# The first batch of a fused attention and expert kernel: which keys come as f32, who issues the hop, and in what order the tensor engine works

## The chip, the cores and the metric

The kernel runs on one core of a Trainium2 chip. Its time is the device time of one launch in microseconds (us). Three runs of the kernel before gave 668.44, 668.48 and 668.60 us; the median, 668.48 us, is the time before.

Five engines have instruction queues of their own: PE (TensorE, matrix multiplies; weight loads beside them), DVE (VectorE), ACT (ScalarE), POOL (GpSimd) and SP (SyncE, which only issues transfers here). POOL issues transfers too. An engine works through its queue in order; an instruction that waits for a semaphore holds everything behind it on that engine.

## The reference, cut to what matters

Two parts in a row. The first is a block-sorted attention for 4 batches of 8 heads with 768 tokens of 64 numbers each: five Sinkhorn rounds turn an 8x8 matrix per head into mixing weights `P`, these mix the 8 blocks (96 tokens each) of keys and values, and every block of queries attends to the mixed block at its own place. The second part is a mixture of 8 experts whose routing weights come from eight Sinkhorn rounds over all 3072 tokens.

```python
for _ in range(5):                       # P = sort_net, (B, H, 8, 8)
    P = exp(P - max(P)); P /= sum(P, -1); P /= sum(P, -2)
k_sorted = einsum('bhij,bhjcd->bhicd', P, k_blocks)   # the same for v
attn = softmax(q_b @ k_sorted_b.T / 8)   # block by block, 96 x 96
x = (attn @ v_sorted_b) as (3072, 512)   # tokens x (heads * 64)
P = routing(x @ w_gate)                  # 8 Sinkhorn rounds over (3072, 8)
out = sum over e of P[:, e] * (relu(x @ w1[e]) @ w2[e])
```

## The kernel before, in words

The batches of the attention are worked one after the other, and the hidden layer and output of expert 0 fill PE beside them (to about 107 us). The experts 1 to 7 follow in one long stage. The order of PE's work is written out by hand: `pin` keeps an instruction in program order on its engine, and strings of short step names are the plan. What is not pinned is placed by the scheduler of the framework.

Batch 0 (to about 36 us) has its own functions, which work on pairs of heads `hp` (0 to 3) and on halves `b` of the eight blocks (blocks 0 to 3 and 4 to 7):

- **Loads.** POOL issues the casting loads (f32 in memory, bf16 on the chip), `load_batch` and `load_w1` (L70 to L102), in the order queries, values, keys of heads 0 to 3, gate weights, first part of `w1`. The keys of heads 4 to 7 are loaded by SP as f32 into a corner of a later buffer (`rawk`, L68) and cast by ACT between the Sinkhorn rounds (L442).
- **Sinkhorn, L437 to L457**: DVE and ACT in turn. `Prep` (L460) copies the result 16 times side by side, split over DVE (4 rows of blocks), ACT (2) and POOL (2); `spread` sends it through PE to 128 partitions; `build_r` (L134) multiplies it with a mask on DVE, four pieces of two heads, giving the weights `Rt`.
- **Values.** `sort_pair` (L272) mixes the values of two heads on PE; DVE or ACT copies them to `vs`. The **hop** (L151) moves `vs` to `vsbt`, so that the 96 tokens of a block stand on 96 partitions: one transfer ("piece") per block, for all 8 heads or for 4. SP issues four pieces (block 0 in two halves, blocks 4 and 5), POOL eight (blocks 1 to 3 in two halves, blocks 6 and 7).
- **A gate.** Behind its last piece POOL copies two numbers out of the arrived pieces of blocks 0 and 1 (L482), and only then issues the next loads: two parts of `w1`, the values of batch 1, and, after the weights of batch 1, its keys and queries, `w2` and the loads of batch 2.
- **Keys, scores, mixes, turns.** `wide_keys` (k) mixes keys, copied by ACT for pairs 0 and 1 and by DVE for pairs 2 and 3; `half_scores` (s) makes scores, ACT takes the exponentials; `half_mix` (m) multiplies with the hopped values, DVE divides (a reciprocal of the sums, then a product into `og`); `half_turn` (t) transposes two pairs; `half_hidden` (h, g) are the two halves of expert 0's hidden layer on these tokens; `v0` to `v3` are `sort_pair` for batch 1, and `l` the routing logits. In the plan at L492 the two digits behind s and m are the half and the pair; behind t, h and g the half and a group. `m10` is thus the first mix that reads blocks 4 to 7, and it reads all four of them.
- **Blank matmuls.** `warm` (L325) multiplies a block of zeros to keep PE busy; the table `unread` says before which steps one stands.
- **PSUM.** All these steps share four buffers (`pair`); a step waits until the copy that reads its buffer's last content is done.

The later batches use `attention` (L364) with a plan of steps q, k, s, m, t, l: `usual` (L577) for batches 2 and 3, woven with expert 0. In batch 2 a step `x0`, a subtraction on DVE for later, stands behind each of q2, q3 and t0.

Of the kernel before, what the change touches and what calls it, by code (L numbers as in the profile page):

```python
# [20 lines left out]
def mkap(t, dims, off=0):  # L21
    return bass.AP(tensor=t.tensor, offset=t.offset + off, ap=dims)
# [3 lines left out]
def kernel(  # L26
# [11 lines left out]
    nc = tc.nc  # L38
    B, H, S, D = 4, 8, 768, 64
    NB, BL = 8, 96  # L40
    N, Dm, E, F = 3072, 512, 8, 1024
# [22 lines left out]
    pin = tc.keep_in_program_order  # L64
    kt, vt, qt = {}, {}, {}
    osbl = {0: xtp.tile([128, 18, Dm], F32, name="osbl0")}
    rawk = osbl[0].rearrange("p t d -> p (t d)")[:, 0:1536].rearrange("p (h x) -> p h x", h=4)
    nc.sync.dma_start(out=rawk, in_=k[0, 4:8].rearrange("h (p kk) d -> p h (kk d)", kk=6))  # L68

    def load_batch(bb, parts):  # L70
        for x, l0, n in parts:
# [24 lines left out]
    load_batch(0, [("q", l0, 4) for l0 in (0, 4)])  # L96
    Ibig = ones.tile([128, 128], BF16)
    make_identity(nc, Ibig)
    load_batch(0, [("v", 0, 4), ("v", 4, 4), ("k", 0, 4)])
    wg = ones.tile([128, 4, E], BF16)  # L100
    pin(nc.gpsimd.dma_start(out=wg, in_=moe_w_gate.rearrange("(kk k) e -> k kk e", k=128)))
    load_w1(0, 0, 384)  # L102
# [6 lines left out]
    VW = NB * 520  # L109
    vsbt = [perp.tile([128, VW], BF16, name=f"vsb{n}") for n in range(2)]  # L110
# [23 lines left out]
    def build_r(bb, eng, n, pbps=None):  # L134

        Rt[bb] = perp.tile([128, 8, 8, 16], BF16, name=f"R{bb % 2}")
        for h in range(0, 8, n):
            ins = eng.tensor_tensor(
                out=mkap(Rt[bb], [Rt[bb].ap[0], [16, 8 * n], [1, 16]] if pbps is None else
                         [Rt[bb].ap[0], [128, n], [16, 8], [1, 16]], off=h * 128),  # L140
                in0=(mkap(Pb, [Pb.ap[0], [1, 8 * n], [0, 16]], off=(bb * 8 + h) * 8)
                     if pbps is None else
                     mkap(pbps, [pbps.ap[0], [1, n], [32, 8], [0, 16]], off=h)),
                in1=mkap(mask16, [mask16.ap[0], [0, 8 * n], [1, 16]] if pbps is None else
                         [mask16.ap[0], [0, n], [0, 8], [1, 16]]),
                op=ALU.mult)
            if eng is nc.gpsimd:
                pin(ins)


    def hop(bb, pieces=None):  # L151
        for eng, i, h0, n in pieces or [(nc.gpsimd if i % 2 and bb > 1 else nc.sync, i, 0, 8)
# [116 lines left out]
        if 3 in ks:  # L269
            nc.vector.tensor_copy(glog[:, bb * TB:(bb + 1) * TB, :], gp[bb])  # L270

    def sort_pair(bb, hp, pair):  # L272
        t = pair()
        warm(t, bb == 0 and hp == 0)
        for h in range(2):
            pin(nc.tensor.matmul(t[:, h, 0:384], Rt[bb][:, 2 * hp + h].rearrange("p i c -> p (i c)"),
                                 vt[bb][:, 2 * hp + h, :], start=True, stop=True))
        (nc.vector.tensor_copy if (hp % 2 == 0 if bb else hp % 2) else nc.scalar.copy)(
            vs[:, :, 2 * hp:2 * hp + 2, 0:64],
            t[:, :, 0:384].rearrange("p h (kk d) -> p kk h d", d=64))  # L280

    def wide_queries(hp, pair):
        qT[0, hp] = sp.tile([128, 128, 6], BF16, name="qTs", bufs=4)
# [144 lines left out]
    with tc.tile_pool(name="ps0", bufs=4, space=bass.MemoryType.PSUM,  # L428
                      reuse_waits="tile") as ps0:
        pair = lambda: ps0.tile([128, 2, 512], F32, name="pair")  # L430
        warm(pair(), 11)
        rs = pp.tile([32, 8], F32)
        cs = pp.tile([32, 8], F32)
        Pt = P.rearrange("p i j -> p j i")
        nc.vector.reduce_max(out=rs, in_=P, axis=AX.X)
        nc.vector.tensor_sub(P, P, mkap(rs, [rs.ap[0], rs.ap[1], [0, 8]]))
        for it in range(5):  # L437


            pin(nc.scalar.activation(out=P, in_=P, func=AF.Exp))  # L440
            if it in (1, 2):
                pin(nc.scalar.copy(kt[0][:, 2 * it + 2:2 * it + 4], rawk[:, 2 * it - 2:2 * it]))  # L442
            if it == 3:
                warm(pair(), 3)
            for hp in {3: (0, 1), 4: (2, 3)}.get(it, ()):
                wide_queries(hp, pair)
            if it == 1:
                pin(nc.vector.reduce_sum(out=mask16, in_=Ibig.rearrange("p (j c) -> p c j", c=16),
                                         axis=AX.X))
            pin(nc.vector.reduce_sum(out=rs, in_=P, axis=AX.X))  # L450
            nc.vector.reciprocal(out=rs, in_=rs)
            nc.vector.tensor_mul(P, P, mkap(rs, [rs.ap[0], rs.ap[1], [0, 8]]))
            nc.vector.reduce_sum(out=cs, in_=Pt, axis=AX.X)
            if it == 0:
                nc.vector.tensor_scalar_add(cs, cs, 1e-9)
            nc.vector.reciprocal(out=cs, in_=cs)
            nc.vector.tensor_mul(Pt, Pt, mkap(cs, [cs.ap[0], cs.ap[1], [0, 8]]))  # L457

        Prep = perp.tile([32, 8, 8, 16], BF16, name="R1")
        for eng, i0, n in ((nc.vector.tensor_copy, 0, 4), (nc.scalar.copy, 4, 2),  # L460
                           (nc.gpsimd.tensor_copy, 6, 2)):
            pin(eng(Prep[:, i0:i0 + n], mkap(P, [P.ap[0], [8, n], [1, 8], [0, 16]], off=i0 * 8)))

        def spread(n):
            t = pair()
            warm(t, n)
            pbps = t[:, 0, 0:256].rearrange("p (i g) -> p i g", i=8)
            for i in range(8):
                pin(nc.tensor.matmul(pbps[:, i, :], Prep[:, i].rearrange("p j c -> p (j c)"),
                                     Ibig[0:32, 0:32], start=True, stop=True))  # L470
            return pbps

        build_r(0, nc.vector, 2, spread(9))
        S_, G_ = nc.sync, nc.gpsimd
        for hp in range(4):
            sort_pair(0, hp, pair)
            if hp == 1:
                hop(0, [(S_, 0, 0, 4), (G_, 1, 0, 4), (G_, 2, 0, 4), (G_, 3, 0, 4)])
        wide_keys(0, pair)
        hop(0, [(S_, 0, 4, 4), (G_, 1, 4, 4), (G_, 2, 4, 4), (G_, 3, 4, 4),  # L480
                (S_, 4, 0, 8), (S_, 5, 0, 8), (G_, 6, 0, 8), (G_, 7, 0, 8)])
        gate = nc.gpsimd.tensor_copy(  # L482
            held, mkap(vsbt[0], [[VW, 96], [520, 2]], off=259))
        with tc.issue_after(gate.ins):
            load_w1(0, 384, 640)
            load_w1(0, 640, F)
            load_batch(1, [("v", 0, 8)])
        wide_keys(1, pair)
        halves = [mps.tile([128, 8, 384], BF16, name="hTs") for _ in range(2)]
        unread = {"s03": 1, "m01": 1, "m02": 1, "m03": 1}  # L490
        part = {}
        for x in ("s00 k2 s01 k3 p s02 s03 m00 s10 m01 s11 m02 t00 m03 s12 m10 t01 s13 h00 m11 "  # L492
                  "g00 m12 h01 g01 m13 t10 h02 g02 t11 h03 g03 v0 v1 v2 v3 h10 g10 l").split():
            n = [int(c) for c in x[1:]]
            if x[0] == "s":
                half_scores(*n, pair, unread.get(x, 0))
            elif x[0] == "m":
                half_mix(*n, pair, unread.get(x, 0))
            elif x[0] == "t":
                half_turn(*n, lambda: ps0.tile([128, 2048], BF16, name="pair"),  # L500
                          nc.vector.tensor_copy if x == "t11" else nc.scalar.copy)
            elif x[0] == "h":
                part[x[1:]] = t = pair()
                half_hidden(*n, (0, 1), t)
            elif x[0] == "g":
                b, g, t = *n, part[x[1:]]
                half_hidden(b, g, (2, 3), t)
                nc.scalar.activation(out=halves[b][:, 2 * g:2 * g + 2, 0:384],
                                     in_=t[:, :, 0:384], func=AF.Relu)
            elif x[0] == "v":  # L510
                sort_pair(1, *n, pair)
            elif x[0] == "k":
                wide_keys(*n, pair)
            elif x[0] == "l":
                logits(0, lambda shape, dt: pair()[:, 0, 0:TB * E].rearrange(
                    "p (t e) -> p t e", e=E), range(4))
            else:
                nc.vector.tensor_copy(Pb, spread(0).rearrange("p i g -> p g i"))
                build_r(1, nc.gpsimd, 4)
                load_batch(1, [("k", 0, 8), ("q", 0, 4), ("q", 4, 4)])  # L520
                load_w2(0)
        hop(1)
# [10 lines left out]
    with ExitStack() as c2:  # L533
# [36 lines left out]
                                  "m0 m1,t0 m2,t1 m3,t2 t3,l0 l3")  # L570
        run_both(at1, (1, 1, 1, 0, 1, 0, 0, 1, 0, 1, 0, 2))
        load_batch(2, [(x, 0, 8) for x in "vkq"])
        build_r(2, nc.gpsimd, 4)
        run_both(at1, (2, 1, 1, 1))
        run_both(sort_values(2, bank1), (1, 0, 1, 0, 1))
        run_both(at1, (1, 1))
        usual = "q0,q1,k0 k1,q2,s0 k2,q3,s1 m0 k3,s2 m1,t0 s3 m2,t1 m3 t2 t3,l0 l3"  # L577
        for bb, ns in ((2, (5, 3, 2, 4)), (3, (5, 4, 0, 5))):
            at1 = attention(bb, bank1, usual if bb == 3 else usual.replace(
                "q2", "q2,x0").replace("q3", "q3,x0").replace("t0", "t0,x0"))  # L580
            weave(at1, ex, 5, ns[0])
            if bb + 1 < B:
                load_batch(bb + 1, [(x, 0, 8) for x in "vkq"])
                build_r(bb + 1, nc.gpsimd, 4)
            else:
                load_w1(1)
                sums = sum_w(1)
# [338 lines left out]
```

## Time and profile before

The profiled execution took 668.62 us, 0.14 us over the median; its span from the first to the last instruction is 666.9 us.

| what | value |
|---|---|
| PE busy | 654.7 us, 98% of the span |
| DVE, ACT, POOL busy | 535.6, 300.3, 472.6 us |
| PE's granted clock | full in every slice |
| PE busy from 12 to 25 us | 11.47 of 13.00 us |
| PE busy from 25 to 36 us | 10.95 of 11.00 us |
| PE busy from 36 to 107 us | 70.29 of 71.00 us |
| PE busy from 107 us on | 552.60 of 559.90 us |
| hop pieces of batch 0, issue to landing | 2.4 to 3.9 us, median 3.2 |
| hop pieces of batch 1, issue to landing | 5.6 to 7.6 us, median 6.4 |

A line of the timeline reads: start, length, engine, line of the source, operation, what it writes and reads, shapes, number of instructions, and in brackets how long the engine was idle before and what ended that. The chain of waits is followed back from the last instruction; a stretch on it is on the path that sets the end. DMA queue q0 holds what POOL issues, q1 what SP issues.

### The profile page before, as it was taken

The page shows a single profiled execution, that of the slowest core. Times are in us where ns is not written, and L with a number is a line of the kernel's source. Part 1 is how long each engine was busy: PE and PEld are TensorE (multiplying, and loading weights), DVE is VectorE, ACT ScalarE, POOL GpSimd, SP SyncE. Part 2 cuts the span into 40 slices and gives each one's busy share as a digit, 9 for nine tenths or more (in the row PEclk, how much of TensorE's full clock was granted, in tenths as well). Part 3 has the DMA queues.
Part 4 walks back from the last instruction along what each step waited for, and adds up shares of the span by engine and source line. Part 5 has one row for each costly group of instructions (what it writes and reads, how often), then busy time and mean ns, then how long its engine had stood idle before and what let it go on. Part 6 is the DMA issues. An engine that isn't in the chain of part 4 may idle for free.

```text
span 666.9 us, 13213 instructions
## 1 busy us (share of the span) xinstructions
PE 654.7 (98%) x5063; PEld 434.4 (65%) x5140; DVE 535.6 (80%) x1128; ACT 300.3 (45%) x535; POOL 472.6 (71%) x501
## 2 busy tenths in 40 slices
PE   7999999999999999999999999999999999999997
PEld 3766675554666666666666666666666666666666
DVE  6656876874888888888888888888888888888886
ACT  5775773476455433343333333333433343434330
POOL 4814343037897898898897999689886999646653
PEclk9999999999999999999999999999999999999999
DMA  9998964003042140033003040024003120001124
GB/s 187 175 220 143 149 109 64 1 0 64 1 64 42 24 64 0 1 64 48 17 1 64 2 64 1 11 53 64 1 1 65 20 45 1 1 0 61 68 95 159
DMA packets 33311, 36.96 MB, mean 55 GB/s; under 512 B 2112, under 2 KB 26304, under 8 KB 33248
## 3 DMA queue, kind: packets, MB, share of 16 engines
q0 software_dynamic: 26832, 27.13, 26.0%
q1 hardware_dynamic: 6416, 8.99, 4.3%
q8 instruction: 40, 0.66, 0.4%
q14 instruction: 23, 0.19, 0.1%
HBM read 52.45 MB, written 6.29 MB: 88 GB/s over the span
## 4 chain that ended last, share of the span: by engine, by line
PE 92%; DVE 2%; DMA 2%; ACT 2%; issue 1%; POOL 0%; ACTq 0%; DVEq 0%; POOLq 0%
PE oacc L766 37%; PE bk L678 36%; PE bk L392 3%; PE oacc L401 3%; PE bank L401 3%; PE bank L392 2%; PE bank L240 1%; DMA kvq<-in_q_dram 1%; DVE osbl L731 1%; PE pair L360 1%; DVE h L725 1%; PE bank L200 1%; PE bk L766 1%; ACT hT L721 1%; PE bank L251 1%
## 5 line engine op out<-in xcount | busy, mean ns | idle before, releaser
L731 DVE SCALAR_TENSOR_TENSOR osbl<-oacc,glog,osbl 128x256 f32<-128x256 f32 (+1 forms) x490 | 248.5, 521 | 61.9 <-PE oacc L766 61.9
L678 PE MATMUL bk<-xtT,w1e 128*128 128x512 bf16 x475 | 154.8, 379 | 0.9
L749 POOL TENSOR_TENSOR hs<-hT 128x512 bf16<-128x512 bf16 (+2 forms) x105 | 99.4, 956 | 63.0 <-DVE hT L718 62.9
L766 PEld LDWEIGHTS <-hT 128*128 128x128 bf16 x996 | 97.4, 98 | 62.8 <-issue 0.6
L766 PEld LDWEIGHTS <-hs 128*128 128x128 bf16 x996 | 96.9, 97 | 55.5 <-issue 0.2
L721 ACT ACTIVATE hT<-bk 128x512 bf16<-128x512 f32 x84 | 50.2, 598 | 159.3 <-PE bk L678 141.5
L766 PE MATMUL oacc<-w2e,hT 128*128 128x256 bf16 x796 | 119.6, 273 | 0.5
L749 POOL TENSOR_TENSOR hs<-hs,hT 128x512 bf16<-128x512 bf16 (+2 forms) x105 | 99.2, 952 | 4.8
L749 POOL TENSOR_TENSOR hs<-hT,hs 128x512 bf16<-128x512 bf16 (+2 forms) x105 | 99.0, 951 | 4.9
L678 PE MATMUL bk<-xc,wc 128*128 128x512 bf16 x319 | 96.3, 379 | 0.4
L766 PE MATMUL oacc<-w2e,hs 128*128 128x256 bf16 x612 | 91.7, 272 | 0.7
L707 ACT COPY u<-bk 128x512 f32<-128x512 f32 x84 | 49.3, 587 | 87.9 <-PE bk L678 76.4
L678 PEld LDWEIGHTS <-w1e 128*128 128x128 bf16 x672 | 65.8, 98 | 19.0
L725 DVE SCALAR_TENSOR_TENSOR h<-bk,hT 128x512 bf16<-128x512 f32 x84 | 58.1, 692 | 13.9 <-ACT hT L721 6.8
L715 DVE CUSTOM_DVE_ANT_0 hT<-bk,p 128x512 bf16<-128x512 f32 x84 | 57.3, 682 | 6.8 <-PE bk L678 3.2
L712 ACT COPY p<-bk 128x512 f32<-128x512 f32 x84 | 49.3, 587 | 24.3 <-PE bk L678 24.3
L699 ACT COPY p<-bk 128x512 f32<-128x512 f32 x84 | 49.2, 586 | 20.2 <-PE bk L678 20.2
L703 DVE CUSTOM_DVE_ANT_0 hT<-bk,p 128x512 bf16<-128x512 f32 x84 | 57.3, 682 | 1.1 <-ACT osbl L810 0.8
L718 DVE CUSTOM_DVE_ANT_0 hT<-bk,u 128x512 bf16<-128x512 f32 x84 | 57.3, 682 | 0.5 <-PE bk L678 0.5
L766 PE MATMUL oacc<-w2s,hs 128*128 128x256 bf16 x364 | 54.4, 272 | 0.3
L678 PEld LDWEIGHTS <-wc 128*128 128x128 bf16 x504 | 49.3, 98 | 7.8 <-issue 0.2
L678 PE MATMUL bk<-xtT,wc 128*128 128x512 bf16 x159 | 48.0, 379 | 0.0
(150 smaller groups left out, 837.9 us busy)
## 6 DMA issues: line engine op xcount, KB each, us to landing
w1e<-in_moe_w_dram POOLq DMA_DIRECT2D x7, 1024.0 KB, 8.3
w2e<-in_moe_w_dram POOLq DMA_DIRECT2D x7, 1024.0 KB, 8.8
out_dram<-osbl SPq DMA_DIRECT2D x23, 256.0 KB, 2.3
kvq<-in_v_dram POOLq DMA_DIRECT2D x3, 768.0 KB, 9.8
kvq<-in_k_dram POOLq DMA_DIRECT2D x3, 768.0 KB, 11.1
vsb<-vs SPq DMA_DIRECT2D x18, 97.5 KB, 4.6
kvq<-in_q_dram POOLq DMA_DIRECT2D x4, 384.0 KB, 9.6
kvq<-in_q_dram POOLq DMA_DIRECT2D x2, 768.0 KB, 19.8
```

The lines of the kernel that those rows point to most:

```text
L678: hold(nc.tensor.matmul(ps, wa[:, kk, :], xa[:, kk, :], start=(first and kk == 0), stop=(kk == 1), skip_group_check=True))
L699: still(nc.scalar.copy(p1, u))
L703: nc.vector._custom_dve(TENSOR_ADD_SAT, out=c11, in0=w, in1=p1, s0=TOP, s1=0.0)
L707: still(nc.scalar.copy(u2, u))
L712: still(nc.scalar.copy(p5, v))
L715: nc.vector._custom_dve(TENSOR_ADD_SAT, out=c22, in0=u, in1=p5, s0=TOP, s1=0.0)
L718: nc.vector._custom_dve(TENSOR_ADD_SAT, out=c12, in0=v, in1=u2, s0=TOP, s1=0.0)
L721: still(nc.scalar.activation(out=c21, in_=u, func=AF.Relu))
L725: nc.vector.scalar_tensor_tensor(out=h3[e, p][:, i, :], in0=u, scalar=0.0, in1=c22, op0=ALU.max, op1=ALU.subtract)
L731: nc.vector.scalar_tensor_tensor(out=o, in0=ps, scalar=glog[:, t, e:e + 1], in1=o, op0=ALU.mult, op1=ALU.add)
L749: hold(nc.gpsimd.tensor_tensor(out=c, in0=a, in1=b, op=o))
L766: nc.tensor.matmul(ps, h[:, fb, :], w[:, fb, :], start=(first and fb == 0), stop=(fb == 3), skip_group_check=True)
```

## The change

Of batch 0:

- SP loads the keys of heads 0 to 3 as f32 (ACT casts them), POOL those of heads 4 to 7.
- `Prep` is split 4, 3, 1 over DVE, ACT and POOL.
- `build_r` becomes a generator, and its pieces are pinned: three of them come first, then `sort_pair` 0 to 2, with the fourth piece after the copy of pair 1 on DVE; `wide_keys(0)` comes ahead of `sort_pair` 3, whose PSUM buffer is taken before. The copies to `vs` are pinned.
- Of the second round of the hop, SP issues blocks 0 and 2 (upper heads) and blocks 4 to 7, POOL blocks 1 and 3: seven pieces by SP in all, five by POOL.
- The gate and its copy are gone; the loads stand right behind POOL's last piece.
- In the plan `m03` moves ahead of `t00`, `h10` ahead of `v0`, and `g10` between `v2` and `v3`; the blank matmuls before `m01` and `m03` are gone.

Of batches 2 and 3: in `usual`, `q2` moves ahead of `k1` and `q3` ahead of `k2`. `spread_r` runs the generator through at once for batches 1 to 3, as before.

```diff
-    nc.sync.dma_start(out=rawk, in_=k[0, 4:8].rearrange("h (p kk) d -> p h (kk d)", kk=6))
+    nc.sync.dma_start(out=rawk, in_=k[0, 0:4].rearrange("h (p kk) d -> p h (kk d)", kk=6))
...
-    load_batch(0, [("v", 0, 4), ("v", 4, 4), ("k", 0, 4)])
+    load_batch(0, [("v", 0, 4), ("v", 4, 4), ("k", 4, 4)])
...
         for h in range(0, 8, n):
+            yield
             ins = eng.tensor_tensor(
...
-            if eng is nc.gpsimd:
-                pin(ins)
+            pin(ins)
+
+    def spread_r(bb):
+        for _ in build_r(bb, nc.gpsimd, 4):
+            pass
...
-                pin(nc.scalar.copy(kt[0][:, 2 * it + 2:2 * it + 4], rawk[:, 2 * it - 2:2 * it]))
+                pin(nc.scalar.copy(kt[0][:, 2 * it - 2:2 * it], rawk[:, 2 * it - 2:2 * it]))
...
-        for eng, i0, n in ((nc.vector.tensor_copy, 0, 4), (nc.scalar.copy, 4, 2),
-                           (nc.gpsimd.tensor_copy, 6, 2)):
+        for eng, i0, n in ((nc.vector.tensor_copy, 0, 4), (nc.scalar.copy, 4, 3),
+                           (nc.gpsimd.tensor_copy, 7, 1)):
...
-        build_r(0, nc.vector, 2, spread(9))
+        r0 = build_r(0, nc.vector, 2, spread(9))
         S_, G_ = nc.sync, nc.gpsimd
-        for hp in range(4):
-            sort_pair(0, hp, pair)
-            if hp == 1:
-                hop(0, [(S_, 0, 0, 4), (G_, 1, 0, 4), (G_, 2, 0, 4), (G_, 3, 0, 4)])
+        for hp in (0, 1, 2):
+            next(r0)
+        next(r0)
+        sort_pair(0, 0, pair)
+        sort_pair(0, 1, pair)
+        hop(0, [(S_, 0, 0, 4), (G_, 1, 0, 4), (G_, 2, 0, 4), (G_, 3, 0, 4)])
+        sort_pair(0, 2, pair)
+        last_pair = pair()
+        next(r0, 0)
         wide_keys(0, pair)
-        hop(0, [(S_, 0, 4, 4), (G_, 1, 4, 4), (G_, 2, 4, 4), (G_, 3, 4, 4),
-                (S_, 4, 0, 8), (S_, 5, 0, 8), (G_, 6, 0, 8), (G_, 7, 0, 8)])
-        gate = nc.gpsimd.tensor_copy(
-            held, mkap(vsbt[0], [[VW, 96], [520, 2]], off=259))
-        with tc.issue_after(gate.ins):
-            load_w1(0, 384, 640)
-            load_w1(0, 640, F)
-            load_batch(1, [("v", 0, 8)])
+        sort_pair(0, 3, pair, last_pair)
+        hop(0, [(S_, 0, 4, 4), (G_, 1, 4, 4), (S_, 2, 4, 4), (G_, 3, 4, 4),
+                (S_, 4, 0, 8), (S_, 5, 0, 8), (S_, 6, 0, 8), (S_, 7, 0, 8)])
+        load_w1(0, 384, 640)
+        load_w1(0, 640, F)
+        load_batch(1, [("v", 0, 8)])
         wide_keys(1, pair)
...
-        unread = {"s03": 1, "m01": 1, "m02": 1, "m03": 1}
+        unread = {"s03": 1, "m02": 1}
...
-        for x in ("s00 k2 s01 k3 p s02 s03 m00 s10 m01 s11 m02 t00 m03 s12 m10 t01 s13 h00 m11 "
-                  "g00 m12 h01 g01 m13 t10 h02 g02 t11 h03 g03 v0 v1 v2 v3 h10 g10 l").split():
+        for x in ("s00 k2 s01 k3 p s02 s03 m00 s10 m01 s11 m02 m03 t00 s12 m10 t01 s13 h00 m11 "
+                  "g00 m12 h01 g01 m13 t10 h02 g02 t11 h03 g03 h10 v0 v1 v2 g10 v3 l").split():
...
-        usual = "q0,q1,k0 k1,q2,s0 k2,q3,s1 m0 k3,s2 m1,t0 s3 m2,t1 m3 t2 t3,l0 l3"
+        usual = "q0,q1,k0 q2,k1,s0 q3,k2,s1 m0 k3,s2 m1,t0 s3 m2,t1 m3 t2 t3,l0 l3"
```

More of the change, by code (lines that the diff above doesn't have):

```diff
@@ L270, in logits, with sort_pair @@
             nc.vector.tensor_copy(glog[:, bb * TB:(bb + 1) * TB, :], gp[bb])
-    def sort_pair(bb, hp, pair):
-        t = pair()
+    def sort_pair(bb, hp, pair, t=None):
+        t = t or pair()
         warm(t, bb == 0 and hp == 0)
@@ L277, in sort_pair @@
                                  vt[bb][:, 2 * hp + h, :], start=True, stop=True))
-        (nc.vector.tensor_copy if (hp % 2 == 0 if bb else hp % 2) else nc.scalar.copy)(
-            vs[:, :, 2 * hp:2 * hp + 2, 0:64],
-            t[:, :, 0:384].rearrange("p h (kk d) -> p kk h d", d=64))
+        (pin if bb == 0 else lambda ins: ins)(
+            (nc.vector.tensor_copy if (hp % 2 == 0 if bb else hp % 2) else nc.scalar.copy)(
+                vs[:, :, 2 * hp:2 * hp + 2, 0:64],
+                t[:, :, 0:384].rearrange("p h (kk d) -> p kk h d", d=64)))
     def wide_queries(hp, pair):
@@ L518 @@
                 nc.vector.tensor_copy(Pb, spread(0).rearrange("p i g -> p g i"))
-                build_r(1, nc.gpsimd, 4)
+                spread_r(1)
                 load_batch(1, [("k", 0, 8), ("q", 0, 4), ("q", 4, 4)])
@@ L572 @@
         load_batch(2, [(x, 0, 8) for x in "vkq"])
-        build_r(2, nc.gpsimd, 4)
+        spread_r(2)
         run_both(at1, (2, 1, 1, 1))
@@ L583 @@
                 load_batch(bb + 1, [(x, 0, 8) for x in "vkq"])
-                build_r(bb + 1, nc.gpsimd, 4)
+                spread_r(bb + 1)
             else:
```

## The prediction

> **What bounds the kernel now.** I read the page's busy shares first, then busy time by stretch, then PE's timeline in the first 40 us, then the chain of waits there, and last the transfers.
>
> ```profile
> PE 654.7 (98%) x5063; PEld 434.4 (65%) x5140; DVE 535.6 (80%) x1128; ACT 300.3 (45%) x535; POOL 472.6 (71%) x501
> ...
> 12.00:25.00 13.00, 11.47 (x197) 7.75 (x196) 9.72 (x21) 9.65 (x14) 9.60 (x16) 1.00 1.13 172
> 25.00:36.00 11.00, 10.95 (x131) 7.57 (x130) 5.63 (x11) 7.61 (x10) 7.44 (x10) 1.00 1.30 197
> ```
>
> PE bounds nearly everything (first number behind the comma: PE busy). From 25 us on it hardly pauses, so a shift of the first batch reaches the end unchanged. Only 12 to 25 us has idle time, 1.53 us of it.
>
> ```profile
> 15.48 0.86 PE L301 MATMUL pair<-R,kvq 128*64 128x128 bf16 x24 [0.49 <-DMA kvq<-in_k_dram]
> 16.90 0.38 PE L316 MATMUL pair<-qTs,kTs 64*96 64x96 bf16 x8 [0.56 <-ACT kTs L305]
> ...
> 19.65 0.38 PE L316 MATMUL pair<-qTs,kTs 64*96 64x96 bf16 x8 [0.16 <-DVE kTs L305]
> ...
> 23.82 0.55 PE L336 MATMUL pair<-vsb,atp 96*96 96x65 bf16 x8
> ...
> 25.18 0.82 PE L360 MATMUL pair<-xtT,w1e 128*128 128x384 bf16 x4
> ```
>
> The waits are for the loaded keys (0.49), their copies (0.56, 0.16) and, in the chain, 0.06 for the hop at 22.43. m10, the first mix that needs blocks 4 to 7, ran at 23.82 without waiting; h00 began at 25.18. These two rows are my yardstick.
>
> ```profile
> 17.11 1.53 POOL vsb L154 x3
> 18.65 3.75 DMA vsb<-vs
> 22.43 0.25 PE pair L336 x2
> ```
>
> The last upper piece (block 3) was issued by POOL at 18.65 and landed 3.75 us later, just as m02 wanted it. POOL's eight pieces went out every 0.52 us, SP's four every 0.63 to 1.35. What lands matters more: this is the DMA view of 15 to 20 us, then the q1 line (SP's packets) of four stretches, 16.75 to 18.70, 19.20 to 21.30, 38.45 to 46.42 and 61.85 to 66.80.
>
> ```profile
> vsb<-vs POOLq DMA_DIRECT2D x6, 48.8 KB, 2.9
> vsb<-vs SPq DMA_DIRECT2D x2, 97.5 KB, 3.9
> vsb<-vs POOLq DMA_DIRECT2D x2, 97.5 KB, 3.4
> vsb<-vs SPq DMA_DIRECT2D x2, 48.8 KB, 3.2
> ...
> q1 hardware_dynamic: 224, 0.10, 32.6%
> ...
> q1 hardware_dynamic: 224, 0.20, 42.3%
> ...
> q1 hardware_dynamic: 895, 0.80, 38.4%
> ...
> q1 hardware_dynamic: 448, 0.40, 43.6%
> ```
>
> A piece by SP is 112 packets. So q1 carried 2 pieces in 1.95 us, 2 in 2.10, 8 in 7.97 (loads beside them) and 4 in 4.95: about 1.0 us each whatever their size, one behind the other.
>
> **The change part by part.** *Keys and Prep.* The f32 keys land long before use (ACT cast them at 5.77 and 6.77, and still does two); POOL's keys, landed by 15.43, are now first read by k2 near 16.7, so their wait of 0.49 goes. `Prep`: POOL's cast of two rows took 0.64 (to 12.71, the last that `spread` waited for), ACT's 0.40; three rows on ACT I take as 0.5, one on POOL as 0.4. The first `R` then starts 0.1 earlier (0 to 0.2), at 12.92.
>
> *R and sorting.* DVE makes an `R` piece every 0.33, three by 14.0. sort 0 to 2 start 13.40, 13.73, 14.06; a copy starts 0.53 behind its matmuls (13.50 to 14.03). Pair 1: 14.26 to 15.21 on DVE; fourth `R` to 15.54; sort 3 at 15.59; its copy 16.12 to 17.07. Before it ended at 16.19: the second round of the hop starts 0.88 later.
>
> *Keys and scores.* `wide_keys(0)` needs the PSUM buffer of pair 0 (ACT's copy, 14.74), so 14.78, not 15.48. ACT copies it behind pair 2: 15.36 to 16.17. With k1 in between s00 starts at 16.38 (before 16.90). s03 waits for the DVE copies of k2 and k3, now behind pair 3's: 19.24 (before 19.65). Then by the old pitches (s 0.31, m 0.44 to 0.47, t 0.35, a blank 0.22; two blanks gone): m00 19.55, m02 21.30, m03 21.74, t00 22.18, s12 22.53. m10's buffer waits for m02's product on DVE, which the new order puts behind m03's reciprocal: 23.25. Were the hop there, h00 would follow at 23.25 + 0.44 + 0.68 + 0.31 = 24.68, 0.5 earlier than before.
>
> *The hop.* SP's queue now holds, behind the 17.07 copy, blocks 0 and 2 (upper), 4, 5, 6, 7. First issue 17.15; packets 1.33 later (15.42 to 16.75 before); six pieces at 1.0 us: 24.48; landing 0.6 to 0.9 behind the last packet: block 7 at 25.2. POOL's five end near 18.5, and the upper pieces that m02 needs are there by about 21.4. The bounds for block 7: SP's issue pace of 0.63 with a landing of 3.0, 17.15 + 3.15 + 3.0 = 23.3, no wait; the batch 1 hop beside loads, up to 7.6 from an issue at 20.5, 28.1. The loads now start at 18.5 instead of 20.29 and come in beside blocks 5 to 7. Nearest is the hop of batch 0 itself, so I take 25.2 plus 0.3 for the loads, 25.5. m10 holds PE until then, with t01, s13 and h00 queued behind it and ACT's next exponentials and copies waiting for those: h00 at 25.5 + 0.12 + 0.68 + 0.31 = 26.6. **Term 1: +1.4** (-0.5 to +3.6).
>
> *The gate and the loads.* The gate's copy (0.24) and three issues leave POOL. Loads 1.8 us earlier gain nothing: PE did not pause for the values of batch 1 at 32.13 nor for its keys at 35.70. If they came later instead, the cover is 0.5 and 0.3 us (landed 31.6 and 35.4).
>
> *h10 ahead of v0, v3 behind g10.* Counted from the end of g03: before, v 1.59 (with a wait for DVE), h10 and g10 1.30, l 0.68, first keys of batch 1 at 3.57. Now 0.65 + 0.99 + 0.65 + 0.33 + 0.68 = 3.30. But the built program lets those first keys wait for ACT's copy of v3, which is queued behind g10's activation; the queries and scores of batch 1 stand behind them on PE:
>
> ```profile
> 33.03 1.51 ACT L278 CAST vs<-pair 128x768 bf16<-128x768 f32 x2
> 35.22 0.81 ACT L508 ACTIVATE hTs<-pair 128x768 bf16<-128x768 f32 x1 [0.67 <-PE pair L360]
> ```
>
> g10 ends at 2.29, its activation runs 2.44 to 3.25, the copy ends at 4.05, keys at 4.08. **Term 2: +0.5** (-0.3 to +0.8). SP's hop of batch 1 starts behind that copy too, 1.1 us later against PE. Its last piece landed 46.9, its first reader ran at 48.02: covered, with nothing left; without cover up to 0.4, in the range. POOL's load of the next queries waits for v3 as well; it stood behind 20 us of other loads anyway.
>
> *Queries ahead of keys.* Batch 2 before:
>
> ```profile
> 64.11 0.82 PE L392 MATMUL bank<-xtT,w1e 128*128 128x384 bf16 x4
> 64.86 0.53 PE L200 MATMUL bank<-R,kvq 128*64 128x128 bf16 x12
> 65.32 0.51 PE L186 MATMUL bank<-Ibig,qr 128*128 128x128 bf16 x6
> 65.76 0.56 PE L222 MATMUL bank<-qTs,kTs 64*96 64x96 bf16 x16
> ```
>
> The starts give 0.75 + 0.46 + 0.44 = 1.65. A hidden step that no other array shape follows takes 0.65; q before k 0.43 (0.77 for the twelve at 62.88, less 0.34 for six); k before s 0.46 (70.82 to 71.28). Together 1.54: 0.1 less, four times. ACT gets q2 earlier, which may take 0.1 off the stretched scores (0.61 instead of 0.49 at 67.90). **Term 3: -0.5** (-0.9 to +0.3, since in batch 2 the 1.4 us DVE subtraction now precedes k1's copy, with 0.2 left before s1).
>
> The sum, +1.4, goes on the profiled 668.62, or on its span of 666.9 with 1.7 around it: 670.0. The median is 0.14 lower: **669.9 us**. Within 0.2% (1.3 us) is about what a measurement of this kernel can't tell from no change; this lies just outside.
>
> **The rivals.** *The hop is in time* (not slower): decided at m10; block 7 must land by about 23.5, so q1 must take 0.65 us or less per piece, not 1.0. For it: SP issues every 0.63. Against: none of four stretches was under 0.97. Then -0.5 + 0.5 - 0.5: 668.0. [...]
>
> *The first batch loses all its waits and both blanks* (faster): 0.49 + 0.56 + 0.16 + 0.06 + 0.07 + 0.43 = 1.77 off, again +0.5 - 0.5: 666.7. It needs m10's buffer early as well.
>
> *The loads weigh in full:* in batch 1 a piece took 2.5 us longer beside loads (5.6 against 3.1 at least). Block 7 at 27.7, term 1 at +3.6: 672.1.
>
> **How the numbers follow.** Forecast (own range 669.0 to 671.0) 0.50, of which 0.37 beyond 0.2%; hop in time 0.25, within; all waits gone 0.15, faster; full loads 0.10, slower. So slower 0.47, same 0.38, faster 0.15. The range 667.0 to 671.8 leaves out part of the two outer cases, about 0.16.
>
> **What would show it.** In the profile after: s00 near 16.4 without the key wait; SP's six pieces from 17.1; idle time of about 2 us inside m10 ended by the hop, h00 near 26.6; 0.8 us before the first keys of batch 1, ended by ACT's copy; about 0.1 us less at each query step. I am wrong if m10 starts by 23.5 with its pieces landed, or if the later batches move by more than 1 us.

## The result, and the profile after

The changed kernel takes 674.25 us (median of five runs, 673.17 to 675.22) against 668.48 before: ratio 1.0085, 95% interval 1.0073 to 1.0096. That is 5.8 us slower, outside the range. The profiled execution is the longest of the five, 675.22 us with a span of 673.3; it carries 1.4 us of an early half clock (a stretch in which PE is granted half its full clock; below) that the other four, by their mean clock of 0.994 against its 0.991, do not have.

The page's busy line, and busy time by stretch (duration, PE, PEld, DVE, ACT, POOL, then granted clock, DMA share, GB/s):

```profile
PE 660.5 (98%) x5138; PEld 436.4 (65%) x5138; DVE 534.6 (79%) x1128; ACT 300.1 (45%) x535; POOL 469.8 (70%) x497
```

```profile
0.00:12.00 12.00, 8.97 (x65) 4.22 (x66) 7.76 (x36) 6.86 (x12) 6.05 (x13) 0.90 0.99 184
12.00:25.00 13.00, 11.82 (x181) 7.44 (x180) 9.07 (x19) 8.88 (x13) 7.91 (x12) 0.96 1.03 144
25.00:36.00 11.00, 6.87 (x66) 4.95 (x66) 2.90 (x7) 3.35 (x6) 5.36 (x7) 0.69 1.29 206
```

PE is still busy for 98% of the span, and the sums of the two pages can't be set against each other (they hold 5138 and 5063 records of the nearly same program). The stretches tell it: in 25 to 36 us PE is busy for 6.87 us instead of 10.95, and what it does there is slower work, at a granted clock of 0.69 instead of 1.00. PE's timeline (start, duration, line, [idle before it and what ended it]):

```profile
9.56 1.44 PE L293 MATMUL pair<-Ibig,kvq 128*64 128x128 bf16 x24 [1.05 <-DMA kvq<-in_q_dram]
10.94 3.15 PE L332 MATMUL pair<-blank 128*128 128x512 bf16 x9
...
14.90 1.16 PE L280 MATMUL pair<-kvq,R 128*128 128x384 bf16 x6 [0.20 <-DVE R L139]
...
17.12 0.50 PE L280 MATMUL pair<-kvq,R 128*128 128x384 bf16 x2 [0.29 <-DVE R L139]
...
18.00 0.38 PE L321 MATMUL pair<-qTs,kTs 64*96 64x96 bf16 x8
...
24.69 0.54 PE L341 MATMUL pair<-vsb,atp 96*96 96x65 bf16 x4 [0.17 <-DVE og L347]
29.15 0.29 PE L341 MATMUL pair<-vsb,atp 96*96 96x65 bf16 x2 [3.92 <-DMA vsb<-vs]
29.65 0.29 PE L341 MATMUL pair<-vsb,atp 96*96 96x65 bf16 x2 [0.20 <-DMA vsb<-vs]
...
31.00 1.46 PE L365 MATMUL pair<-xtT,w1e 128*128 128x384 bf16 x4
...
43.19 0.53 PE L204 MATMUL bank<-R,kvq 128*64 128x128 bf16 x12 [0.69 <-ACT vs L283]
```

Read it from the top. The queries of 9.56 and most of the nine blanks behind them run at half speed (the trace's record of the clock has 0.50 from 9.65 to 13.06 us), and the first sort starts at 14.90 instead of 13.50; nothing ahead of it was edited that PE waits for. From there the front gains: m10 starts 0.87 late, not 1.4. Then m10 waits 3.92 us for block 6 and 0.20 for block 7, and h00 (31.00) is 5.8 us later than before. It takes 1.46 us for four matmuls that took 0.82: half clock. The keys of batch 1 wait 0.69 for ACT's copy of v3.

The budget of the span, +6.4, comes out of these starts: +1.4 early half clock; -0.5 the front up to m10; +4.1 wait in m10; +2.1 half clock behind it (m10 to h00 is 6.31 instead of 1.36, of which 4.12 are waits, so 0.83; and the rest, 1.24, between h00 and the last step of the batch); +0.4 at the keys (0.69 less the 0.27 that the forecast gave the order); -1.1 in later batches (+7.5 at the keys of batch 1 and at the first output step, 53.77 against 46.30; +6.4 at the end).

The wait is not found on the chain of waits this time: that chain leaves PE at 15.75 for POOL's issues and ends in a load of `w2`. PE's own waits in 12 to 36 us have it:

```profile
PE pair L341 <- DMA vsb<-vs: 4.1, 2, 3.9
```

The DMA view of 20 to 25 us (issues: KB each, median us from issue to landing), and its queue lines of 22 to 24 and of 24 to 26 us (packets, MB, share of the engines; q0 carries POOL's transfers, q1 SP's):

```profile
vsb<-vs SPq DMA_DIRECT2D x4, 97.5 KB, 6.0
w1e<-in_moe_w_dram POOLq DMA_DIRECT2D x1, 384.0 KB, 8.4
w1e<-in_moe_w_dram POOLq DMA_DIRECT2D x1, 256.0 KB, 5.5
vsb<-vs POOLq DMA_DIRECT2D x1, 48.8 KB, 3.1
...
q0 software_dynamic: 276, 0.14, 77.1%
q1 hardware_dynamic: 146, 0.12, 31.1%
...
q0 software_dynamic: 487, 0.30, 117.9%
q1 hardware_dynamic: 41, 0.04, 7.2%
```

Before, pieces of this size took 3.2 to 3.9. The four issued here took 6.0 in the middle; the last two, issued at 21.23 and 21.99, took 7.9 and 7.6. In 24 to 26 us SP's queue moved 41 packets, a third of a piece (112), while the loads moved 487.

### The profile page after: what moved, and what is told of

Read it like the earlier page. It is cut to its first block, busy times and chain, and to the rows that moved or that the text cites. A ratio compares the mean times of both kernels' runs of the same rounds, so it can differ in the third digit from the quotient of the medians.

```text
span 673.3 us, 13284 instructions
## 1 busy us (share of the span) xinstructions
PE 660.5 (98%) x5138; PEld 436.4 (65%) x5138; DVE 534.6 (79%) x1128; ACT 300.1 (45%) x535; POOL 469.8 (70%) x497
## 4 chain that ended last, share of the span: by engine, by line
PE 94%; DMA 3%; POOL 1%; issue 1%; DVE 0%; ACT 0%; ACTq 0%; POOLq 0%
PE bk L686 38%; PE oacc L774 37%; PE bk L397 3%; PE bank L406 3%; PE oacc L406 3%; PE bank L397 2%; DMA w2e<-in_moe_w_dram 2%; PE bank L244 1%; DMA kvq<-in_q_dram 1%; PE bank L204 1%; PE bank L226 1%; PE bk L774 1%; PE bank L255 1%; POOL kvq L75 1%; PE bk L810 1%
## 5 line engine op out<-in xcount | busy, mean ns | idle before, releaser
L686 PE MATMUL bk<-xtT,w1e 128*128 128x512 bf16 x504 | 162.6, 379 | 0.0
L686 PE MATMUL bk<-xc,wc 128*128 128x512 bf16 x336 | 99.9, 379 | 0.0
L686 PE MATMUL bk<-xtT,wc 128*128 128x512 bf16 x168 | 50.0, 379 | 0.0
## 6 DMA issues: line engine op xcount, KB each, us to landing
vsb<-vs SPq DMA_DIRECT2D x20, 97.5 KB, 5.0
```

The source lines that it names most:

```text
L686: hold(nc.tensor.matmul(ps, wa[:, kk, :], xa[:, kk, :], start=(first and kk == 0), stop=(kk == 1), skip_group_check=True))
```

## The experiments

My theory after the result: blocks 6 and 7 are late because they stand on SP's queue while POOL's loads are already running; the wait then drops PE's clock. Rivals: the missing gate, the later sorted copy, a slow SP queue in itself. In each comparison the kernel before ran on the same chip; its medians were 668.80 to 668.84.

### The gate back

```
-        load_w1(0, 384, 640)
-        load_w1(0, 640, F)
-        load_batch(1, [("v", 0, 8)])
+        gate = nc.gpsimd.tensor_copy(held, mkap(vsbt[0], [[VW, 96], [520, 2]], off=259))
+        with tc.issue_after(gate.ins):
+            load_w1(0, 384, 640)
+            load_w1(0, 640, F)
+            load_batch(1, [("v", 0, 8)])
```

> The changed kernel with POOL's gate put back: the three loads wait for the lower pieces of blocks 0 and 1, as before. Theory (the queue): blocks 6 and 7 are late because they stand on SP's queue, and POOL's loads, which start before the last of SP's packets, take the DMA engines. The gate opens when the lower pieces land, near 19.8, and the loads' first issue was at 20.23 without it, so nothing changes: m10 still waits about 4 us, 673 to 675 us. Rival (the gate): the gate kept the loads off the hop; with it back m10 waits under 1 us and the time is 668 to 670.

Measured: 674.80 us, ratio 1.0084 (1.0069 to 1.0099). PE's timeline of m10:

```profile
24.46 0.24 PE L341 MATMUL pair<-vsb,atp 96*96 96x65 bf16 x2 [0.82 <-DMA vsb<-vs]
28.53 0.29 PE L341 MATMUL pair<-vsb,atp 96*96 96x65 bf16 x2 [3.83 <-DMA vsb<-vs]
...
29.88 1.46 PE L365 MATMUL pair<-xtT,w1e 128*128 128x384 bf16 x4
```

The early half clock is absent here (granted clock 1.00 in 0 to 12 us), and the wait is as long (0.82 and 3.83 us), with h00 at 29.88. The gate's return alone mends nothing.

### The three pieces back on POOL

```
-        hop(0, [(S_, 0, 4, 4), (G_, 1, 4, 4), (S_, 2, 4, 4), (G_, 3, 4, 4),
-                (S_, 4, 0, 8), (S_, 5, 0, 8), (S_, 6, 0, 8), (S_, 7, 0, 8)])
+        hop(0, [(S_, 0, 4, 4), (G_, 1, 4, 4), (G_, 2, 4, 4), (G_, 3, 4, 4),
+                (S_, 4, 0, 8), (S_, 5, 0, 8), (G_, 6, 0, 8), (G_, 7, 0, 8)])
```

> The changed kernel with the upper piece of block 2 and blocks 6 and 7 issued by POOL again, ahead of its loads, and still no gate. Theory (the queue): the pieces of POOL go out before its loads and land within 3.3 us of their issue, m10 waits less than 0.5 us, PE keeps its full clock, and the time is 667.5 to 669.5. Rival (the gate, or the later sorted copy): m10 still waits 2 us or more, 671 or over.

Measured: 668.22 us, ratio 0.9998 (0.9986 to 1.0010): 6 us of the loss are gone, without a gate. Seven of ten executions lie between 667.79 and 668.71; the other three have a mean clock of 0.997 or less, and the profiled one is the longest of them, 671.06. Its timeline around m10 and its stretch of 25 to 36 us:

```profile
22.46 0.60 PE L341 MATMUL pair<-vsb,atp 96*96 96x65 bf16 x10 [0.28 <-DMA vsb<-vs]
...
23.91 0.79 PE L341 MATMUL pair<-vsb,atp 96*96 96x65 bf16 x8 [0.20 <-DVE og L347]
24.52 0.83 PE L356 MATMUL pair<-Ibig,og 96*128 96x96 bf16 x8
...
25.76 1.46 PE L365 MATMUL pair<-xtT,w1e 128*128 128x384 bf16 x4
```

```profile
25.00:36.00 11.00, 11.00 (x91) 7.21 (x89) 3.90 (x8) 5.31 (x7) 5.50 (x7) 0.73 1.28 193
```

m10 does not wait for the hop any more. But this execution lost 3 us to half clock with PE never idle for more than 0.3 us at a time: from 24.0 to 30.85 us everything runs at half speed. In 20.6 to 24.0 PE was busy 2.88 of 3.40 us; in the kernel before, which has a blank more in m01 and in m03, 3.34.

### The loads held until the pieces have landed

```
+        gate = nc.gpsimd.tensor_copy(held, mkap(vsbt[0], [[VW, 96], [520, 2]], off=6 * 520 + 519))
+        with tc.issue_after(gate.ins):   # the same three loads
```

> The changed kernel, all its pieces by SP, but the three loads held until blocks 6 and 7 have landed. Theory (loads beside the pieces): without loads the last two pieces land 3 to 4 us behind their issue instead of 7.6 to 7.9, so m10 waits under 1.5 us; the columns of w1 that h01 reads then land about 3 us later than before and may cost up to 2 us: 668 to 671. Rival (SP's queue is slow by itself with six pieces): the two still land 7 us behind their issue, m10 waits 4 us, and with the loads later still the time is 675 or over.

Measured: 671.52 us, ratio 1.0045 (1.0028 to 1.0061), 0.5 above the expected range. The DMA view of 19 to 23.3 us with SP's pieces, SP's queue in 20 to 22 us, and PE's timeline:

```profile
vsb<-vs SPq DMA_DIRECT2D x4, 97.5 KB, 2.8
...
q1 hardware_dynamic: 324, 0.30, 82.1%
```

```profile
24.45 0.82 PE L365 MATMUL pair<-xtT,w1e 128*128 128x384 bf16 x4
...
27.72 1.15 PE L365 MATMUL pair<-xtT,w1e 128*128 128x384 bf16 x6 [0.78 <-DMA w1e<-in_moe_w_dram]
30.63 1.15 PE L365 MATMUL pair<-xtT,w1e 128*128 128x384 bf16 x6 [0.74 <-DMA w1e<-in_moe_w_dram]
34.88 1.14 PE L280 MATMUL pair<-kvq,R 128*128 128x384 bf16 x6 [0.81 <-DMA kvq<-in_v_dram]
38.65 0.53 PE L204 MATMUL bank<-R,kvq 128*64 128x128 bf16 x12 [1.08 <-DMA kvq<-in_k_dram]
```

Without loads beside them the same pieces of the same queue take 2.8 us, 0.69 us each (324 packets in 2 us), and block 7 lands at 23.20. m10 does not wait at all and h00 starts at 24.45, 0.73 earlier than before. So SP's queue is not slow. What was won is lost again, since the held loads are now late four times: 0.78 + 0.74 + 0.81 + 1.08 = 3.4 us.

### Blanks in m10's wait

```
-        unread = {"s03": 1, "m02": 1}
+        unread = {"s03": 1, "m02": 1, "m10": 20}
```

> The changed kernel with 20 blank matmuls (0.22 us each, 4.3 us) ahead of m10's own, so that PE is busy while it waits for blocks 6 and 7. Theory (the clock adds to the wait): the granted clock, 0.69 over 25 to 36 us in the changed kernel, stays near 1.00, the blocks behind m10 take their usual times, and the time falls by 1.5 to 2 us, to 672.2 to 672.8. Rival (the wait is all of it): the time stays within 0.5 us of 674.25 or grows.

Measured: 672.15 us (671.94 to 672.39), ratio 1.0049 (1.0034 to 1.0064): 2.1 us less than the changed kernel, 2.4 by the two ratios. PE's timeline, and the stretch of 25 to 36 us:

```profile
23.20 4.49 PE L332 MATMUL pair<-blank 128*128 128x512 bf16 x19 [0.18 <-DVE og L347]
...
28.33 0.23 PE L341 MATMUL pair<-vsb,atp 96*96 96x65 bf16 x2 [0.23 <-DMA vsb<-vs]
...
29.15 0.82 PE L365 MATMUL pair<-xtT,w1e 128*128 128x384 bf16 x4
```

```profile
25.00:36.00 11.00, 10.76 (x109) 7.15 (x108) 4.12 (x9) 4.63 (x6) 3.88 (x5) 1.00 1.31 207
```

Block 7 comes as late as with the gate back (28.29 against 28.49), but the clock stays at 1.00 and h00's four matmuls take 0.82. Useless work in the wait saves 2.1 us: that is the price of the clock, apart from the wait.

### The kernel before with SP's pieces only

The diff of the second experiment, reversed, on the kernel before: gate, order and all else stay.

> The kernel before with one edit: the upper piece of block 2 and blocks 6 and 7 go from POOL to SP's queue; gate, order and all else as before. Theory (the queue): SP issues blocks 6 and 7 near 20 to 21 us, when POOL's loads have begun (its own pieces end earlier, so the gate opens near 19.8); the two land near 28, m10 waits 3.5 to 4.5 us and part of the next 4 us runs at half clock: 673 to 675 us. Rival (it takes the missing gate or the later sorted copy as well): the pieces land before 25, 668.5 to 670.

Measured: 669.91 us, ratio 1.0023 (1.0000 to 1.0047). The expectation of 673 to 675 is missed, and the median lies in the rival's range: two of ten executions took 675, the others 668.97 to 671.32. The profiled one is one of the two; its clock was 0.90 in 0 to 12 us, and its m10 shows the wait:

```profile
26.77 0.29 PE L336 MATMUL pair<-vsb,atp 96*96 96x65 bf16 x2 [1.57 <-DMA vsb<-vs]
28.64 0.29 PE L336 MATMUL pair<-vsb,atp 96*96 96x65 bf16 x2 [1.57 <-DMA vsb<-vs]
```

So the queue alone makes the loss possible, not certain: of the 84 executions of the kernel before that ran beside the experiments one took 674.17 (mean clock 0.989, not traced), all others under 671.1. Something else in the change makes it come in all five executions.

### The gate alone taken out of the kernel before

```
-        gate = nc.gpsimd.tensor_copy(
-            held, mkap(vsbt[0], [[VW, 96], [520, 2]], off=259))
-        with tc.issue_after(gate.ins):   # the three loads stay, without it
```

> The kernel before with only the gate taken out: the three loads are issued right behind POOL's last piece. Theory (the queue): POOL's pieces are ahead of the loads on the same queue, and the gate, open at once when POOL reached it at 20.17, held nothing back; no change, 668.2 to 669.0 us. Rival (the gate protects the hop): the upper pieces and blocks 5 to 7 land 1 us or more later, 669.5 or over.

Measured: 668.66 us, ratio 1.0000 (0.9991 to 1.0009). With the last pieces on POOL's own queue, ahead of the loads, taking the gate out changes nothing that can be measured. It held little back there: the first load is issued at 20.14 instead of 20.29.

### The end of batch 0 alone

```
-  h03 g03 v0 v1 v2 v3 h10 g10 l
+  h03 g03 h10 v0 v1 v2 g10 v3 l
```

> The kernel before with only the order at the end of batch 0 changed: h10 ahead of v0, v3 behind g10. Prediction's term 2: the first keys of batch 1 wait 0.7 to 0.8 us for ACT's copy of v3, against 0.27 won by the order: +0.5, 668.7 to 669.3 us. Rival (the wait hides behind something later): 668.3 to 668.6.

Measured: 668.81 us, ratio 0.9998 (0.9989 to 1.0006). PE's timeline at the first keys of batch 1:

```profile
35.69 0.53 PE L200 MATMUL bank<-R,kvq 128*64 128x128 bf16 x12 [0.30 <-DVE glog L270]
```

The time lies in the expected range, but not for the expected reason. Alone, this order makes the keys wait 0.30 for the copy of the logits, not 0.7 for v3's, and the 0.27 it wins cancel that: 35.69 against 35.70. In the changed kernel the wait is for v3's copy (0.69 above). Which PSUM buffer the first keys get is thus not the same in the two; why was not followed up.

### The queries ahead of the keys alone

```
-        usual = "q0,q1,k0 k1,q2,s0 k2,q3,s1 m0 k3,s2 m1,t0 s3 m2,t1 m3 t2 t3,l0 l3"
+        usual = "q0,q1,k0 q2,k1,s0 q3,k2,s1 m0 k3,s2 m1,t0 s3 m2,t1 m3 t2 t3,l0 l3"
```

> The kernel before with only the queries put ahead of the keys in batches 2 and 3. Prediction's term 3: -0.5, 0.1 per step, 667.9 to 668.2 us. By the trace of the changed kernel the later batches regain 1.1 us (+7.5 at the first output step, +6.4 at the end); if the swap does it, 667.2 to 667.6. Rival (what is regained is slack left by the long wait, not the swap): 668.4 to 668.7.

Measured: 667.91 us, ratio 0.9988 (0.9980 to 0.9996). PE's timeline in batch 2, and the first steps of batch 3 and of the next part:

```profile
64.08 0.82 PE L392 MATMUL bank<-xtT,w1e 128*128 128x384 bf16 x4
...
66.12 0.82 PE L392 MATMUL bank<-xtT,w1e 128*128 128x384 bf16 x4
...
67.67 0.56 PE L222 MATMUL bank<-qTs,kTs 64*96 64x96 bf16 x16
68.16 0.82 PE L392 MATMUL bank<-xtT,w1e 128*128 128x384 bf16 x4
...
85.19 0.83 PE L186 MATMUL bank<-Ibig,qr 128*128 128x128 bf16 x12
...
106.03 2.11 PE L392 MATMUL bk<-xtT,w1e 128*128 128x384 bf16 x12
```

The first round of hidden step, queries, keys and scores takes 2.04 instead of 2.14, the second 2.04 instead of 2.26: the scores that stretched to 0.61 take 0.49 again (67.67 to 68.16). Batch 3 starts 0.47 earlier, the next part 0.86 earlier. This is the one part of the change that wins.

### Old order of the first sorts, in the changed kernel

```
-        last_pair = pair()
-        next(r0, 0)
+        sort_pair(0, 3, pair)
         wide_keys(0, pair)
-        sort_pair(0, 3, pair, last_pair)
```

(All pieces of `R` are made ahead of the sorts, too.)

> The changed kernel with its first part as before: all four pieces of R and all four sorts ahead of the first keys. SP's second round then starts 0.9 us earlier, at 16.9, and blocks 6 and 7 are issued near 19.5 and 20.2 as in the kernel before with SP's pieces (668.9 to 670.1 in 8 of 10 executions, +0.9 by the medians). POOL, without a gate, issues its first load near 18.7 and its second near 19.5. Theory (it is decided by how far the loads are on when SP's last pieces are issued; the second load's issue comes ahead of both): blocks 6 and 7 still take 6 us or more, m10 waits over 2.5 us: 672 to 675. Rival (the later copy of pair 3 alone loses the race; the missing gate does not matter): 668.3 to 670.3.

Measured: 673.93 us, ratio 1.0073 (1.0053 to 1.0093). PE's timeline of m10:

```profile
26.06 0.29 PE L341 MATMUL pair<-vsb,atp 96*96 96x65 bf16 x2 [2.56 <-DMA vsb<-vs]
28.48 0.29 PE L341 MATMUL pair<-vsb,atp 96*96 96x65 bf16 x2 [2.13 <-DMA vsb<-vs]
```

Undoing the later copy does not mend it either, as undoing the gate did not. The kernel before with SP's pieces has both undone, and there most executions are free of the loss; but it has the rest of the change undone too, so no run shows that these two are enough.

### Four blanks where PE waits for the queries

In each of three kernels `wide_queries` puts four blanks ahead of the third group:

```
         t = pair()
+        warm(t, 4 if hp == 2 else 0)
```

With SP's pieces on the kernel before:

> The kernel before with blocks 6 and 7 and the upper piece of block 2 on SP, as in the run before, and 4 blank matmuls between the second and the third group of queries. Two of ten executions of that run took 675, and the profiled one of them showed half the clock from 9.5 to 13.4 us. Theory: that is what delays its front by 1.4 us and puts SP's last pieces behind the loads; with the blanks the clock holds, all executions lie between 668.9 and 670.3, and the trace shows blocks 6 and 7 landed by about 25, with m10 waiting 0.5 to 1.5 us. Rival (the race between pieces and loads is lost by chance, whatever the clock): executions of 674 and over remain, or all of them get there.

Measured: 669.33 us, ratio 1.0016 (1.0004 to 1.0028). Ten of twelve executions lie between 669.10 and 669.86, two at 672.60 and 673.15. The profiled one is the latter; its clock is 1.00 in 0 to 12 us, and m10 shows

```profile
24.41 0.24 PE L337 MATMUL pair<-vsb,atp 96*96 96x65 bf16 x2 [0.43 <-DMA vsb<-vs]
25.90 0.29 PE L337 MATMUL pair<-vsb,atp 96*96 96x65 bf16 x2 [1.25 <-DMA vsb<-vs]
```

The half clock of that earlier trace ends at 12.9, not at 13.4 (its clock is 0.96 in 12 to 25 us). No execution took 675, as my theory had it, but 0 of 12 against 2 of 10 is too few to show that. The expectation that all lie below 670.3 is missed, and the rival holds in part: the race between pieces and loads is now and then lost without the early half clock. With waits of 1.7 us together the clock came down here too: it is 0.69 over 25 to 36 us, which is half the clock for about 6.8 of them, and h00's four matmuls take 1.46.

With the queries ahead of the keys on the kernel before:

> The kernel before with two edits: queries ahead of keys in batches 2 and 3, and 4 blank matmuls between the second and the third group of queries. Theory: the swap alone gave 667.9; the blanks run while PE waits for a load, cost nothing and take away the executions with a clock of 0.997 (one in five of the kernel before, 1.2 us longer): 667.6 to 668.0, all within 0.8 us. Rival (the early half-clock stretch does not depend on PE's work between 8.5 and 9.5 us): executions above 669 remain.

Measured: 668.05 us, ratio 0.9990 (0.9981 to 0.9998); ten of eleven executions within 0.83 us, one at 669.19. No clock under 0.999 in these eleven, where 10 of the 84 executions of the kernel before had 0.997 or less.

With all that the earlier runs had shown to cost undone, and the front and the swap kept:

> The changed kernel with four edits: block 2's upper piece and blocks 6 and 7 back on POOL; the blanks of m01 and m03 back; the old order at the end of batch 0 (values, then h10 and g10); and 4 blank matmuls between the second and the third group of queries, where PE waits for their load. What is left of the change is the front, the missing gate and the swap. Theory: the kernel with POOL's pieces took 667.8 in undisturbed executions, the wait of 0.70 before the first keys of batch 1 less the 0.27 that the new order won goes, and no execution shows the half-clock stretch that three of ten showed: 667.2 to 667.7, all within 0.8 us. Rival (front and tail are worth nothing, and the half-clock stretch has another cause): 667.8 to 668.3, with executions above 669.

Measured: 668.15 us, ratio 0.9988 (0.9979 to 0.9997); eleven executions between 667.91 and 668.53, none with a clock under 0.999. The expectation of 667.2 to 667.7 is missed. PE's timeline:

```profile
24.94 0.82 PE L366 MATMUL pair<-xtT,w1e 128*128 128x384 bf16 x4
...
32.21 1.46 PE L280 MATMUL pair<-kvq,R 128*128 128x384 bf16 x8 [0.17 <-DMA kvq<-in_v_dram]
...
36.16 0.53 PE L204 MATMUL bank<-R,kvq 128*64 128x128 bf16 x12 [0.32 <-ACT hTs L517]
```

h00 is 0.24 earlier than before, and then the values of batch 1 are not there (0.17) and its keys wait 0.32 for an activation. Nor is the 0.24 the front's: in the run above, without the front, h00 is at 24.97, and the values are waited for too (0.15). The front wins nothing that reaches the end: with it 668.15, without it 668.05. The only three versions whose interval lies below that of the kernel before (the swap alone, with the blanks, and this one) all have the swap; they win about 0.1%.

### The runs side by side

Issues and landings from the traces, in us; "order" is that of the first sorts. All have blocks 6 and 7 on SP.

| kernel | second load issued | block 6 issued, landed | block 7 issued, landed | waits in m10 |
|---|---|---|---|---|
| changed (early half clock) | 21.01 | 21.23, 29.11 | 21.99, 29.61 | 4.12 |
| gate back, new order | 20.14 | 19.83, 24.42 | 20.52, 28.49 | 4.65 |
| no gate, new order, blanks in m10 | 19.52 | 19.75, 27.82 | 20.51, 28.29 | 0.23, behind the blanks |
| no gate, old order | 19.43 | 19.35, 26.01 | 20.21, 28.44 | 4.69 |
| gate and old order, early half clock | 20.93 | 20.94, 26.73 | 21.67, 28.60 | 3.14 |
| gate and old order, blanks (its longest execution) | 20.34 | 19.49, 24.37 | 20.19, 25.86 | 1.68 |
| loads held | 24.26 | 19.81, 22.57 | 20.49, 23.20 | 0 |

Of these pieces, one issued after POOL's second load takes 5.8 to 8.2 us to land, one issued 0.1 us ahead of it 5.7 or 6.7, one issued 0.3 to 0.9 ahead 4.6 to 4.9, and one without loads 2.7 or 2.8. The second and third rows come nearest to a test of this alone: up to m10 they differ by the gate, the second load is 0.6 us later with it, and block 6 lands 4.6 instead of 8.1 us behind its issue. With the old order the second load is 0.9 us later where the gate is in (19.43 and 20.34), and the old order moves SP's last pieces by 0.3 (20.52 to 20.19 with the gate); the change gave up both, and put on SP the pieces that run in this race.

## Why the prediction was wrong

*Term 1, the hop: wrong, +1.4 forecast, about +6 measured* (in the run with the gate back, the trace with this wait and without the early half clock, h00 is at 29.88, +4.70, and 1.64 of half clock come behind it; with +0.43 at the keys and -0.87 in the later batches that makes the 5.9 by which its span, 672.8, is longer). The step that failed is "block 7 at 25.2 plus 0.3 for the loads". Both numbers in it are off, in opposite directions. Without loads block 7 lands at 23.20 (third experiment): SP's pieces go out at the pace of its issues, 0.64 us, not at 1.0. The 1.0 came from stretches (the fourth of them gives 1.24) in which q1 shared the engines with POOL's pieces or with loads (q0 had 33% to 81% of the engines in them), and in the first of which SP's own issues lay up to 1.35 us apart, so a part of what the loads do was in it already. With loads the landing is 28.49 (the gate back), so they cost 5.3 us, not 0.3. The right row was in the working, the batch 1 hop beside loads with up to 7.6 us from an issue, "28.1"; I kept it as a bound and took the hop of batch 0 as the nearer one. But in batch 0 of the kernel before every piece on POOL is ahead of the loads on the same queue, and SP's last is issued 2.0 us ahead of the first load. The nearest row is the one with the same neighbours, not the one of the same batch.

*The clock: left out.* The sum had the wait, but no price for PE standing idle, and it took the two dropped blanks as pure gain. Blanks in the wait gave back 2.1 us. In the changed kernel the clock is 0.50 from 9.65 to 13.06 us (3.41) and from 26.72 to 33.55 (6.83). The second stretch begins 1.5 us behind PE's last matmul, at 25.23, and lasts 3.9 us beyond the landing of block 7 at 29.61. But PE need not stand idle for it: in the run with POOL's pieces the clock fell at 24.0 behind a stretch of 3.40 us with PE busy for 2.88, and it stayed at half to 30.85 with PE busy all the while. What sets when it falls and when it comes back, no run here shows.

*The front: right in its times, wrong in its worth.* m10's buffer was forecast for 23.25; m10 started at 23.28 (the gate back) and 23.27 (the loads held). s00 was forecast for 16.38; it was at 16.60 (the gate back). With the hop in time h00 was forecast at 24.68 and came at 24.45. But of this gain nothing reached the end: the loads of batch 1 have 0.5 and 0.3 us in hand, the cover that the working named for another case, and the gain runs into them.

*The gate: half right.* That earlier loads gain nothing is not contradicted by any run, though without the gate in the kernel before they came only 0.15 earlier. That they cost 0.3 was wrong.

*Term 2, the keys of batch 1: right in the changed kernel.* 0.69 us of wait for ACT's copy of v3, forecast 0.78; net +0.4, forecast +0.5. Alone on the kernel before it is worth 0.0, since there the wait is another one.

*Term 3, the queries: right in direction, too small.* -0.86 in the trace, -0.5 forecast, inside the given -0.9 to +0.3. The four rounds gave the forecast 0.1 each. The stretched scores were priced at 0.1 once; they gave 0.12 in batch 2 and 0.18 in batch 3 (91.35 less 90.68 before, 90.49 less 90.00 with the swap), and the mix behind them in batch 2 another 0.11, which the working did not have.

*The rivals.* "The hop is in time" has the right rate of SP's queue and the wrong neighbours: by 23.5, its own condition, only the run with the loads held had them of those with blocks 6 and 7 on SP. The issuing engine alone does not decide it: without loads SP's pieces of 97.5 KB took 2.8 us, POOL's in the second experiment 3.0 and 3.3; beside the loads SP's took up to 8.2. "The loads weigh in full" (672.1, chance 0.10) was the right mechanism, with 2.5 us for the loads where they take 5.3, and without the clock.

*What is left of the difference.* The early half clock of the profiled execution (1.4 us) need not be of the change: 10 of 84 executions of the kernel before have a mean clock as low as one such stretch makes it (0.997), or lower. None of them was traced; the one trace of it on the kernel before is that with SP's pieces.

## What to carry to other kernels

A transfer that is needed soon belongs ahead of the bulk loads on the loads' own queue: there the last two pieces landed in 2.9 to 3.5 us here, while on another queue, beside loads, they took 4.6 to 8.2, and a few tenths of a microsecond decided which. Price a new wait of the matrix engine with its clock: here 4 us of wait cost 6. And take the duration of a moved transfer from a row with the same neighbours, even if a row of the same loop stands nearer.

## What was not expected of the hardware

- How sharp the race is: block 6 landed 4.6 us behind its issue when that was 0.31 ahead of the second load's, and 6.7 when it was 0.08 ahead. In 24 to 26 us SP's queue got 41 packets through while POOL's got 487.
- The clock fell with PE mostly busy. Busy for 2.88 of the 3.40 us ahead of 24.0 (POOL's pieces, without the blanks of m01 and m03) was followed by 0.50 to 30.85; busy for 1.99 of 3.40 (7.10 to 10.50 in the kernel before) was followed by full clock. So the share of busy time in the profile does not tell by itself when the clock falls, and what does tell is not shown by any run here.
- With those two blanks PE was busy for 3.34 of the 3.40 us from 20.6 to 24.0 in the kernel before, for 3.29 in the version with all mended, and in both the clock was 1.00 from 12 to 36 us.
- Four blanks of 0.22 us in a gap of 1.05 us that PE has anyway cost nothing that can be measured, and in the 22 executions of the two kernels with them that had SP's pieces off the loads' way no mean clock is under 0.999. At the rate of the kernel before, 10 of 84 at 0.997 or less, that would come by chance about once in 16.
- PEclk reads 1.00 in the first microseconds of the kernel before, but the trace's record of the clock begins at 7.24 us there, and the 14 blanks ahead of that take 0.44 us each, where those from 10.85 on start 0.22 us apart: about half the speed.
